# Block 0 of a fused attention and two-layer MoE kernel: weight conversions put in another place of the order

## The chip, the cores and the metric

The kernel runs on one core of one Trainium2 chip. The metric is the device time of one execution in microseconds (us). TensorE (PE), VectorE (DVE), ScalarE (ACT), GpSimd (POOL) and the DMA queue of SyncE (SP) each work through a list of instructions of their own, in the order in which the built program holds it, and wait for one another by semaphores.

## The reference

A sparse attention (four heads with a local window of 32, four with a stride of 32) feeds a gated layer with RMS normalisation, and that a second gated layer. All of it is fp32.

```python
def _attn_ref(q, k, v):                       # 4 x 8 heads x 576 x 64
    scores = scale * np.matmul(q, k.transpose(0, 1, 3, 2))
    rel = pos[:, None] - pos[None, :]
    mask_local = (rel >= 0) & (rel < 32)
    mask_strided = (rel >= 0) & (pos[None, :] % 32 == pos[:, None] % 32)
    masks = np.stack([mask_local if h < H // 2 else mask_strided for h in range(H)], axis=0)
    ...
    return np.matmul(attn, v)

def _moe_ref(x, w_gate, w_val, w_out, rms_g):  # x: 2304 x 512, w: 512 x 1536
    xn = x / rms * rms_g
    g = xn @ w_gate
    silu = g * (1.0 / (1.0 + np.exp(-g)))
    return silu * (xn @ w_val) @ w_out

def _moe2_ref(x, w_a, w_b, w_out):
    return (x @ w_a) * (x @ w_b) @ w_out
```

## The kernel before, in words

The tokens are worked in six blocks of 4 x 96 = 384 (`NB`, `NTB`). For each block the attention gives x, as four pieces of 128 features. A first stage computes, for each of twelve chunks `fc` of 128 hidden features, g = x Wgate and v = x Wval (24 matmuls of 384 columns, since each operand is split into a high part in fp32r and the rest, and three of the four products are taken), h = silu(g / rms) v, and the output sums y (12 matmuls). A second stage after block 5 does the second layer.

The weights arrive in HBM as 64-bit words (the inputs' raw bytes) and are made into the two parts on the chip, in block 0 alone: later blocks keep the gate and value weights `gv` in SBUF, and read the output weights `wo` back from DRAM (`wod`). The **conversion** of a third (128 x 512 numbers) or of a fused pair (128 x 1024) has these steps: `first` on ACT clears a bit pattern of the high word in place (line 134) and makes the three low bits `z` out of the low word (line 139); `second` on DVE joins the two (line 142); `last` casts the high part on ACT (line 147) and subtracts it on POOL (line 148). With a low mode "D" instead of "A" (the table `LOW`), line 136 on DVE makes `z` in place of line 139 on ACT. Chunks 1 to 10 convert gate and value weights as one pair (`FUSEDW`).

Block 0 holds three things at once: its own attention, of which nothing hides the start; the conversions of all weights; and the attention of block 1, whose pieces `attention_slot` puts behind the chunks. Most raw weights have slots of their own; the six last thirds (`wo` of chunks 8 to 11, gate and value of chunk 11) share a pool `raw` of two buffers, so four of their loads wait until the conversion of an earlier third has read its buffer. Behind the last store into `wod` stand the loads of keys for block 2's attention on the same queue.

What sets the order: the program is written in the order of the code, and a scheduler with a model of costs puts each engine's instructions in order before the kernel runs. `tc.issue_after(i)` keeps instructions written inside it behind instruction `i` in that order. `gate(n)` uses it with the n-th row of `GATES`, names of instructions of block 0's attention: `pvm` and `pvr` are the last value product and its sum (lines 278, 281), `sqr` and `snorm` the strided scores' last sum and their normalisation, `norm` the local softmax's, `xhi` the last cast of x, `sqrt` the RMS root (445), `rec` its reciprocal (447). `behind(list)` does the same with a list. `GATES[0]` guards chunk 0's conversion, `GATES[1]` chunk 1's and the first `wo`. The Silu of a chunk is line 751, its product with v line 761, the split of h lines 502 and 503. PSUM tiles of g and v share three banks, so the value product of chunk 1 waits for line 750 of chunk 0 and the gate product of chunk 2 for line 761 of chunk 0.

Of the kernel before, what the change touches and what calls it, by code (L numbers as in the profile page):

```python
# [10 lines left out]
F32 = mybir.dt.float32  # L11
# [4 lines left out]
ALU = mybir.AluOpType  # L16
# [9 lines left out]
NFC = FF // 128  # L26
# [17 lines left out]

GATES = ["pvm snorm sqr",
         "norm pvm snorm sqr",
         "pvr snorm xhi",
         "snorm sqr sqrt xhi",
# [18 lines left out]

LOW = ["AAA"] * NFC
NEG = -1000000000.0
# [5 lines left out]
def fused_kernel(ctx: ExitStack, tc: tile.TileContext, qtl, ktl, vl, qs, ks, vs, cst, w1, w2, out):  # L75
# [5 lines left out]
    nc = tc.nc  # L81
# [102 lines left out]
    def attention(t, pool, psum, banks):  # L184
# [173 lines left out]
        def ptc(g):  # L358
            def f():
                rows, n, keys, units = GROUPS[g]  # L360
                k0 = 0 if g < 2 else 64
                src = st["pps", g][k0:k0 + n].rearrange("k (u h r) -> k u h r", h=2, r=rows // 2)
                for hf in range(2) if g == 2 else [g]:
                    dst = pts[hf][k0:k0 + n, :, :, k0:k0 + rows // 2]
                    nc.scalar.copy(dst, src[:, 4 * hf:4 * hf + 4] if g == 2 else src)
            return f
# [13 lines left out]
        def xhl(i, src):  # L380

            xx = act.tile([128, 2, NTB], F32R, tag="x", name="xx", bufs=8)
            hi, lo = xx[:, 0], xx[:, 1]
            st["xhi"] = nc.scalar.activation(hi, src, AF.Copy, scale=g_sb[:, i:i + 1])
            sq(i)()
            st["xlo"] = nc.vector.scalar_tensor_tensor(lo, src, g_sb[:, i:i + 1], hi.bitcast(F32), op0=ALU.mult, op1=ALU.subtract)
            xt[t, i] = xx
# [99 lines left out]
    def tmp(name):  # L487
        return act.tile([128, NTB], F32, tag="t", name=name, bufs=NTMP)

    made = []  # L490

# [44 lines left out]
    def load_late(which):  # L536
        raw.update(zip(which, load_pair(w1, which, pool)))
# [182 lines left out]
    for t in range(NB):  # L720
# [10 lines left out]
        for fc in range(NFC):  # L731
# [6 lines left out]
            if t == 0 and fc + 1 < NFC:  # L738
                with gate(fc + 1):
                    convert1(fc + 1)  # L740
                if fc + 2 == NFC:
                    load_late([(NFC - 2, 2), (NFC - 1, 2)])
# [20 lines left out]
            if t == 0:  # L763
                wt = wo[0, fc] = wo_tile()
                with gate(fc + 1):
                    run(conversion(raw.pop((fc, 2)), wt, pool, engine(WLO[fc][2]), LOW[fc][2], True))
# [3 lines left out]
                if fc == NFC - 3:  # L770
                    load_late([(NFC - 1, 0), (NFC - 1, 1)])
            prev = (t, fc)
    emit_y(*prev)
# [239 lines left out]
```

## Time and profile before

| what | value |
|---|---|
| median of 3 runs | 982.59 us (980.43, 982.59, 1163.71) |
| the profiled execution's own time | 981.18 us |
| its span, first to last instruction | 979.4 us |
| PE busy, weight loads busy | 944.5 us (96%), 896.9 us (92%) |
| DVE, ACT, POOL busy | 625.2 us (64%), 429.3 us (44%), 537.6 us (55%) |
| mean granted clock of PE | 0.99 |

The page gives the whole span; what the change touches lies in its first 150 us, so it is read there by stretches (windows) and by single instructions in order of time (timelines). A timeline row gives the start, the duration, the engine, the line, the operation, output and inputs, shape and count, and in brackets how long the engine had idled and who ended that. A row of the windows gives the window, its length, then the busy time and instructions of PE, of its weight loads, of DVE, ACT and POOL (of PE and its loads alone, or fewer, where one engine was asked for), the granted clock as a share of the full one, the busy share of the DMA engines and GB/s.

### The profile page before, as it was taken

The numbers are of one execution on the slowest core, as the hardware profiler recorded it, in microseconds if no ns is written. First come the engines' busy times: TensorE is split into PE (matmuls) and PEld (weight loads), VectorE is DVE, ScalarE is ACT, GpSimd is POOL, SyncE is SP. The second block draws the span as 40 slices with busy tenths as digits, with TensorE's granted clock in tenths as the row PEclk, the third lists the DMA queues.
The fourth block names the chain that finished last, engine by engine and source line by source line (L and its number), as shares of the span: only waits on it lengthen the run. The fifth ranks groups of instructions, "written<-read, shape, count | busy, mean of one in ns | idle before, by whom it ended". The sixth has DMA issues, their size and how long they took to land.

```text
span 979.4 us, 14348 instructions
## 1 busy us (share of the span) xinstructions
PE 944.5 (96%) x5438; PEld 896.9 (92%) x5438; DVE 625.2 (64%) x903; ACT 429.3 (44%) x800; POOL 537.6 (55%) x406
## 2 busy tenths in 40 slices
PE   5799999999999999999998999999999999999998
PEld 4699889999999999999998999899999999999996
DVE  5578757648917885887566657666656655465534
ACT  5989645243534433433455555435335423122110
POOL 4488846558739776968346544755643424123211
PEclk7989999999999999999999999999999999999999
DMA  9953376435534553532687975897893973863701
GB/s 347 407 231 119 114 282 210 147 117 177 187 108 134 200 168 110 173 121 80 213 343 302 344 281 206 318 417 319 337 366 138 356 293 113 284 248 150 269 11 65
DMA packets 57364, 215.57 MB, mean 220 GB/s; under 512 B 5968, under 2 KB 14544, under 8 KB 51664
## 3 DMA queue, kind: packets, MB, share of 16 engines
q1 hardware_dynamic: 57296, 214.66, 59.9%
q8 instruction: 43, 0.70, 0.3%
q14 instruction: 25, 0.20, 0.1%
HBM read 172.17 MB, written 42.47 MB: 219 GB/s over the span
## 4 chain that ended last, share of the span: by engine, by line
PE 69%; DVE 10%; DMA 7%; ACT 6%; POOL 4%; issue 4%; SPq 0%; POOLq 0%; DVEq 0%; ACTq 0%
PE o L892 5%; PE o L894 5%; PE o L893 5%; PE Y L838 4%; PE Y L837 4%; PE Y L836 4%; PE y L478 3%; PE v_ps L478 3%; PE y L479 3%; PE y L480 3%; PE v_ps L480 3%; PE g_ps L478 3%; PE v_ps L479 3%; PE g_ps L480 3%; PE g_ps L479 3%
## 5 line engine op out<-in xcount | busy, mean ns | idle before, releaser
L148 POOL TENSOR_TENSOR hl<-c,hl 128x384 fp32r<-128x384 f32 x72 | 79.8, 1109 | 185.7 <-ACT hl L147 180.1
L245 POOL TENSOR_TENSOR prod<-kv_t,qs_t 128x512 f32<-128x512 f32 (+12 forms) x57 | 107.7, 1913 | 17.8 <-DMA kv_t<-in_ks 5.9
L478 PE MATMUL g_ps<-xx,gv 128*128 128x384 f32 x288 | 98.2, 341 | 5.1 <-DVE h L761 5.1
L843 DVE TENSOR_TENSOR c<-c,Y 128x384 f32<-128x384 f32 x108 | 59.3, 551 | 67.5 <-PE Y L838 59.7
L478 PE MATMUL v_ps<-xx,gv 128*128 128x384 f32 x288 | 97.7, 339 | 2.6 <-DVE sg L750 2.1
L479 PE MATMUL y<-hl,wo 128*128 128x384 f32 x288 | 96.1, 338 | 4.0 <-DVE hl L503 4.0
L479 PE MATMUL v_ps<-xx,gv 128*128 128x384 f32 x288 | 98.1, 341 | 0.0
L278 POOL TENSOR_TENSOR prod<-kv_t,S_t 128x512 f32<-128x512 f32 (+12 forms) x57 | 84.8, 1500 | 23.9 <-issue 7.4
L480 PE MATMUL v_ps<-xx,gv 128*128 128x384 f32 x288 | 97.5, 339 | 0.0
L480 PE MATMUL g_ps<-xx,gv 128*128 128x384 f32 x288 | 97.3, 338 | 0.0
L479 PE MATMUL g_ps<-xx,gv 128*128 128x384 f32 x288 | 97.1, 338 | 0.0
L480 PE MATMUL y<-hl,wo 128*128 128x384 f32 x288 | 94.8, 337 | 0.0
L503 POOL TENSOR_TENSOR hl<-h,hl 128x384 fp32r<-128x384 f32 x58 | 62.8, 1083 | 47.8 <-ACT hl L502 41.3
L281 DVE TENSOR_REDUCE xs_t<-prod 128x64 f32<-128x448 f32 (+17 forms) x57 | 85.2, 1515 | 6.0 <-POOL prod L278 5.8
L478 PE MATMUL y<-hl,wo 128*128 128x384 f32 x288 | 85.6, 343 | 1.1 <-ACT wo L147 0.9
L892 PE MATMUL o<-slab,hl 128*128 128x512 f32 x216 | 84.7, 393 | 1.0 <-DVE slab L901 0.5
L893 PE MATMUL o<-slab,hl 128*128 128x512 f32 x216 | 84.6, 392 | 0.0
L894 PE MATMUL o<-slab,hl 128*128 128x512 f32 x216 | 83.5, 395 | 0.0
L147 ACT CAST hl<-c 128x384 fp32r<-128x384 f32 x72 | 37.0, 513 | 104.1 <-DVE c L873 103.9
L751 ACT ACTIVATE sg<-sg 128x384 f32<-128x384 f32 x72 | 37.9, 526 | 90.9 <-DVE sg L750 80.3
L838 PE MATMUL Y<-slab,form 128*128 128x384 f32 x216 | 73.1, 338 | 0.0
L837 PE MATMUL Y<-slab,form 128*128 128x384 f32 x216 | 73.0, 338 | 0.0
(135 smaller groups left out, 2515.5 us busy)
## 6 DMA issues: line engine op xcount, KB each, us to landing
form<-formd SPq DMA_DIRECT2D x32, 1792.0 KB, 10.7
wo<-wod SPq DMA_DIRECT2D x60, 512.0 KB, 3.5
raw<-in_w SPq DMA_DIRECT2D x42, 512.0 KB, 6.9
gv_raw<-in_w SPq DMA_DIRECT2D x30, 512.0 KB, 10.0
formd<-form SPq DMA_DIRECT2D x6, 1792.0 KB, 6.8
formd<-forms SPq DMA_DIRECT2D x6, 1792.0 KB, 11.8
slab<-x2d SPq DMA_DIRECT2D x24, 384.0 KB, 4.5
wod<-wo SPq DMA_DIRECT2D x12, 512.0 KB, 3.3
```

What stands on the lines that cost most here:

```text
L148: lo_eng.tensor_tensor(lo, x, hi.bitcast(F32), op=ALU.subtract)
L245: nc.gpsimd.tensor_tensor(pr, st["ks", g][:, :, :n, :], st["qs"][:, heads(g), mm:mm + 1, :].to_broadcast([128, G, n, D]), op=ALU.mult)
L278: st["pvm"] = nc.gpsimd.tensor_tensor(pr, st["vs", g][:, :, :n, :], st["S"][:, heads(g), mm, :n, None].to_broadcast([128, G, n, D]), op=AL ...
L281: st["pvr"] = nc.vector.tensor_reduce(st["xs"][:, mm, heads(g), :], pr.rearrange("p g n d -> p g d n"), axis=X, op=ALU.add)
L478: nc.tensor.matmul(out_ps, w_hi, x_hi, start=start, stop=False)
L479: nc.tensor.matmul(out_ps, w_hi, x_lo, start=False, stop=False)
L480: nc.tensor.matmul(out_ps, w_lo, x_hi, start=False, stop=stop)
L837: nc.tensor.matmul(bank(n), hi, x[p][:, 1, c], start=False, stop=False, skip_group_check=not begins)
L838: nc.tensor.matmul(bank(n), lo, x[p][:, 0, c], start=False, stop=c == 1, skip_group_check=not begins)
L892: nc.tensor.matmul(o, h[:, 0, cols], w[0], start=n == 0, stop=False)
L893: nc.tensor.matmul(o, h[:, 0, cols], w[1], start=False, stop=False)
L894: nc.tensor.matmul(o, h[:, 1, cols], w[0], start=False, stop=n == len(chunks) - 1)
```

## The change

Five edits. Chunk 0's conversion is also put behind `ptc1`, ACT's copy of the second transposed local weights, and chunk 1's behind `ptc2`, the last of those copies (`GATES`, and `ptc` notes its instruction). Chunk 2's is put behind the RMS root. The low bits of chunks 1 and 2 are made by DVE, for gate and value weights (`LOW`). In `xhl` DVE's low part of x is written ahead of the square. The first `wo` takes row 2 of `GATES` instead of row 1. And every conversion of chunk `fc + 1` and of `wo` `fc` is put behind the product and the split of chunk `fc - 2` (`h_made`).

```diff
--- before.py
+++ after.py
@@ -42,9 +42,9 @@
           "ptc2 pv0 pvc0 pv1 pvc1 xst0 xst1 xstc0 id36 xstc1 rms rinv")
 WARM = 20
 
-GATES = ["pvm snorm sqr",
-         "norm pvm snorm sqr",
-         "pvr snorm xhi",
+GATES = ["pvm snorm sqr ptc1",
+         "norm pvm snorm sqr ptc2",
+         "snorm sqr sqrt xhi",
          "snorm sqr sqrt xhi",
          "rec sexp snorm sqrt xhi"]
 
@@ -65,7 +65,7 @@
 WLO = ["PPP", "PPP", "PPP", "PPP", "PPP", "PPP",
        "PPP", "PPP", "PPP", "PPP", "PPP", "PPD"]
 
-LOW = ["AAA"] * NFC
+LOW = ["AAA", "DDA", "DDA"] + ["AAA"] * 9
 NEG = -1000000000.0
 BIG = 3.0e38
 SCALE = 1.0 / 8.0
@@ -362,7 +362,7 @@
                 src = st["pps", g][k0:k0 + n].rearrange("k (u h r) -> k u h r", h=2, r=rows // 2)
                 for hf in range(2) if g == 2 else [g]:
                     dst = pts[hf][k0:k0 + n, :, :, k0:k0 + rows // 2]
-                    nc.scalar.copy(dst, src[:, 4 * hf:4 * hf + 4] if g == 2 else src)
+                    st[f"ptc{g}"] = nc.scalar.copy(dst, src[:, 4 * hf:4 * hf + 4] if g == 2 else src)
             return f
 
         def pv(p):
@@ -382,8 +382,8 @@
             xx = act.tile([128, 2, NTB], F32R, tag="x", name="xx", bufs=8)
             hi, lo = xx[:, 0], xx[:, 1]
             st["xhi"] = nc.scalar.activation(hi, src, AF.Copy, scale=g_sb[:, i:i + 1])
+            st["xlo"] = nc.vector.scalar_tensor_tensor(lo, src, g_sb[:, i:i + 1], hi.bitcast(F32), op0=ALU.mult, op1=ALU.subtract)
             sq(i)()
-            st["xlo"] = nc.vector.scalar_tensor_tensor(lo, src, g_sb[:, i:i + 1], hi.bitcast(F32), op0=ALU.mult, op1=ALU.subtract)
             xt[t, i] = xx
 
         def xsplit(i, src):
@@ -487,6 +487,7 @@
     def tmp(name):
         return act.tile([128, NTB], F32, tag="t", name=name, bufs=NTMP)
 
+    h_made = {}
     made = []
 
     @contextmanager
@@ -736,7 +737,7 @@
             v_ps = psum.tile([128, 512], F32, tag="gv", name="v_ps", bufs=3)
             mm_in(v_ps[:, :NTB], gv[fc], 1, x)
             if t == 0 and fc + 1 < NFC:
-                with gate(fc + 1):
+                with gate(fc + 1), behind(h_made.get(fc - 2, [])):
                     convert1(fc + 1)
                 if fc + 2 == NFC:
                     load_late([(NFC - 2, 2), (NFC - 1, 2)])
@@ -762,13 +763,15 @@
             hl[t, fc] = split(h, engine(HLO0[fc] if t == 0 else HLO[t]))
             if t == 0:
                 wt = wo[0, fc] = wo_tile()
-                with gate(fc + 1):
+                with gate(max(fc + 1, 2)), behind(h_made.get(fc - 2, [])):
                     run(conversion(raw.pop((fc, 2)), wt, pool, engine(WLO[fc][2]), LOW[fc][2], True))
                 nc.sync.dma_start(wod[fc], wt.rearrange("p a n -> p (a n)").bitcast(F32))
                 if fc % 2:
                     load_units(1)
                 if fc == NFC - 3:
                     load_late([(NFC - 1, 0), (NFC - 1, 1)])
+            if t == 0:
+                h_made[fc] = list(made)
             prev = (t, fc)
     emit_y(*prev)
     evac_y(NB - 1)
```

Where the instructions stand now, at two places. On ACT, behind the square root of the RMS in block 0 (`gv_raw_170` holds the first two `wo` thirds, `173`, `176`, `182`, `185`, `191` the pairs of chunks 1 to 5, `179`, `188` later `wo` thirds; `sg_452` is chunk 0's Silu). Before:

```order
L134 ACTIVATE gv_raw_182<-gv_raw_182 128x1024
L139 ACTIVATE cz_597<-gv_raw_182 128x1024
L134 ACTIVATE gv_raw_179<-gv_raw_179 128x512
L134 ACTIVATE gv_raw_185<-gv_raw_185 128x1024
L139 ACTIVATE cz_684<-gv_raw_185 128x1024
L134 ACTIVATE gv_raw_179<-gv_raw_179 128x512
L134 ACTIVATE gv_raw_188<-gv_raw_188 128x512
L139 ACTIVATE cz_650<-gv_raw_179 128x512
L134 ACTIVATE gv_raw_188<-gv_raw_188 128x512
L134 ACTIVATE gv_raw_191<-gv_raw_191 128x1024
L147 CAST gv_595<-cz_597 128x2x512
L751 ACT_TABLE_LOAD
```

In the changed kernel:

```order
L134 ACTIVATE gv_raw_170<-gv_raw_170 128x512
L139 ACTIVATE cz_481<-gv_raw_170 128x512
L134 ACTIVATE gv_raw_176<-gv_raw_176 128x1024
L134 ACTIVATE gv_raw_170<-gv_raw_170 128x512
L147 CAST wo_479<-cz_481 128x512
L147 CAST gv_513<-cz_515 128x2x512
L752 ACT_TABLE_LOAD
L752 ACTIVATE sg_452<-sg_452 128x384
```

The eleven conversion steps ahead of the Silu's table load have become six, and they are those of the first two `wo` and of chunk 2, which stood ahead of the square root before.

On DVE, at the end of block 0 (`raw_200`, `raw_202`, `raw_1246`, `raw_1248` are the late raw thirds; `prod_1033` and `prod_1133` the last value products of block 1's strided attention, `sg_1198` and `sg_1293` chunks 9 and 10). Before:

```order
L142 SCALAR_TENSOR_TENSOR cz_1159<-raw_200,cz_1159 128x512
L281 TENSOR_REDUCE xs_t_959<-prod_1033 128x128
L750 TENSOR_TENSOR sg_1198<-g_ps_1165,rinv_404 128x384
L435 TENSOR_TENSOR sq_1203<-sq_1203,sq_1063 128x384
L281 TENSOR_REDUCE xs_t_959<-prod_1133 128x128
L761 TENSOR_TENSOR h_1233<-sg_1198,v_ps_1178 128x384
L142 SCALAR_TENSOR_TENSOR cz_1278<-raw_1246,cz_1278 128x512
L503 TENSOR_TENSOR hl_1235<-h_1233,hl_1235 128x384
L142 SCALAR_TENSOR_TENSOR cz_1240<-raw_202,cz_1240 128x512
L750 TENSOR_TENSOR sg_1293<-g_ps_1250,rinv_404 128x384
```

In the changed kernel:

```order
L751 TENSOR_TENSOR sg_1293<-g_ps_1250,rinv_404 128x384
L281 TENSOR_REDUCE xs_t_959<-prod_1033 128x128
L281 TENSOR_REDUCE xs_t_959<-prod_1133 128x128
L435 TENSOR_TENSOR sq_1215<-sq_1215,sq_1203 128x384
L142 SCALAR_TENSOR_TENSOR cz_1159<-raw_200,cz_1159 128x512
L762 TENSOR_TENSOR h_1314<-sg_1293,v_ps_1263 128x384
L447 RECIPROCAL rinv_1300<-rms_t_1298 128x384
L142 SCALAR_TENSOR_TENSOR cz_1240<-raw_202,cz_1240 128x512
L142 SCALAR_TENSOR_TENSOR cz_1278<-raw_1246,cz_1278 128x512
L142 SCALAR_TENSOR_TENSOR cz_1281<-raw_1248,cz_1281 128x512
```

The first join of a late third has moved from ahead of the last two sums (line 281) and of chunk 9's `sg` to behind both sums, chunk 10's `sg` and the last sum of squares, and the others have moved behind the reciprocal.

On PE, the four matmuls that add up the squares for the RMS stand so now: the third behind the 12 matmuls of g of chunk 0, the fourth behind six more of v; before, the last two stood behind seven of each.

## Rows read from the trace of the kernel before

**Rows 1.** Windows by stage: length, busy us (x count) per engine, clock, DMA
```profile
37.98:48.20 10.22, 5.69 (x32) 5.05 (x30) 6.01 (x5) 10.20 (x13) 3.49 (x3) 1.00 1.04 405
48.20:73.60 25.40, 24.23 (x139) 23.91 (x140) 17.75 (x25) 22.59 (x43) 22.16 (x14) 0.87 0.61 236
73.60:98.73 25.13, 24.52 (x166) 23.44 (x165) 21.27 (x27) 23.65 (x44) 22.26 (x15) 1.00 0.33 116
98.73:128.36 29.63, 27.46 (x161) 24.82 (x160) 20.91 (x24) 19.78 (x36) 24.01 (x18) 1.00 0.40 142
...
300.00:400.00 100.00, 100.00 (x630) 98.27 (x629) 81.53 (x105) 39.73 (x64) 77.88 (x49) 1.00 0.45 150
```
**Rows 2.** Window of PE alone after its long pause: length, busy us, clock, DMA
```profile
50.00:52.00 2.00, 2.00 (x8) 0.50 1.08 399
```
**Rows 3.** Timeline of PE: start, us, instruction, [idle before it <- what ended that]
```profile
42.27 0.45 PE L478 MATMUL v_ps<-xx,gv 128*128 128x384 f32 x1 [0.95 <-DVE sg L750]
...
49.37 0.69 PE L478 MATMUL g_ps<-xx,gv 128*128 128x384 f32 x1 [4.75 <-DVE h L761]
...
54.98 0.36 PE L480 MATMUL v_ps<-xx,gv 128*128 128x384 f32 x1
...
57.09 0.33 PE L479 MATMUL g_ps<-xx,gv 128*128 128x384 f32 x1
```
**Rows 4.** Timeline of ACT, from the RMS square root to the first Silu
```profile
37.50 0.58 ACT L445 ACTIVATE rms_t<-att,eps_sb 128x384 f32<-128x384 f32 x1 [0.47 <-PE att L433]
37.98 1.16 ACT L134 ACTIVATE gv_raw<-gv_raw 128x1024 f32<-128x1024 f32 x1
39.00 1.15 ACT L139 ACTIVATE cz<-gv_raw 128x1024 uint32<-128x1024 uint16 x1
...
46.91 1.28 ACT L751 ACT_TABLE_LOAD   x1
48.20 0.52 ACT L751 ACTIVATE sg<-sg 128x384 f32<-128x384 f32 x1
```
**Rows 5.** Timeline of DVE: two joins, x's low parts, the first normalisation
```profile
27.54 1.23 DVE L142 SCALAR_TENSOR_TENSOR cz<-gv_raw,cz 128x1024 uint32<-128x1024 uint32 x1 [1.91 <-ACT cz L139]
...
35.47 1.13 DVE L386 SCALAR_TENSOR_TENSOR xx<-att,cst_sb,xx 128x384 fp32r<-128x384 f32 x2
38.12 2.55 DVE L447 RECIPROCAL rinv<-rms_t 128x384 f32<-128x384 f32 x1 [1.51 <-ACT rms_t L445]
...
41.66 0.55 DVE L750 TENSOR_TENSOR sg<-g_ps,rinv 128x384 f32<-128x384 f32 x1
...
85.39 2.81 DVE L142 SCALAR_TENSOR_TENSOR cz<-gv_raw,cz 128x1024 uint32<-128x1024 uint32 x1
```
**Rows 6.** Groups of DVE by line and shape, 0 to 140 us: xcount | busy us, mean ns | idle before
```profile
L343 DVE TENSOR_SCALAR lsm<-lsm 128x4 f32<-128x4 f32 x4 | 2.4, 594 | 0.0
```
**Rows 7.** Timeline of POOL: first and last value products of the strided attention for block 1
```profile
95.89 2.26 POOL L278 TENSOR_TENSOR prod<-kv_t,S_t 128x512 f32<-128x512 f32 x2 [0.57 <-POOL hl L503]
...
111.31 1.47 POOL L278 TENSOR_TENSOR prod<-kv_t,S_t 128x768 f32<-128x768 f32 x1
```
**Rows 8.** Timeline of DVE at the same place
```profile
111.87 1.46 DVE L142 SCALAR_TENSOR_TENSOR cz<-raw,cz 128x512 uint32<-128x512 uint32 x1 [1.15 <-ACT cz L139]
...
115.77 1.54 DVE L281 TENSOR_REDUCE xs_t<-prod 128x128 f32<-128x768 f32 x1
```
**Rows 9.** Timeline of the DMA queue there, loads of the last raw weights and of block 2's keys
```profile
113.36 0.33 SPq L108 DMA_DIRECT2D raw<-in_w  x1
...
134.98 1.22 SPq L233 DMA_DIRECT2D kv_t<-in_ks  x2
```
**Rows 10.** Timeline of ACT: the first late third that had to wait for its load
```profile
116.97 0.68 ACT L134 ACTIVATE raw<-raw 128x512 f32<-128x512 f32 x1 [1.42 <-DMA raw<-in_w]
```
**Rows 11.** Timeline of PE: first product of block 1 and its first pause
```profile
126.92 0.44 PE L478 MATMUL g_ps<-xx,gv 128*128 128x384 f32 x1
...
144.68 0.45 PE L478 MATMUL v_ps<-xx,gv 128*128 128x384 f32 x1 [1.17 <-DVE sg L750]
```

## The prediction

> **What bounds the kernel now.** I read the windows first. From 300 to 400 us PE is busy all the time [rows 1]. In such a stretch a lead or a lag of PE at the end of block 0 goes straight into the time. The reordered instructions stop differing early in block 2, so the question is only when PE gets block 0 off its hands. In the four windows of block 0, from 37.98 to 128.36 us, PE idles 90.4 - 81.9 = 8.5 us, and it is slowed as well: the granted clock of the second window is 0.87 [rows 1].
>
> The timeline of PE shows where. It waits 4.75 us for chunk 0's product h [rows 3], which waits for the Silu at 48.20 [rows 4]. After that pause the clock stands at 0.50, the lower of the two levels (1.2 GHz) [rows 2]: 17 starts of matmuls from 49.37 to 54.98 take 0.33 us each, then twelve from 54.98 to 57.09 take 0.176 [rows 3]. So the pause costs 4.75 + 17 x 0.154 = 2.6, together 7.4 us. A pause of 0.95 us at 42.27 [rows 3] left no such trace: the clock of the first window is 1.00 [rows 1].
>
> The reader is to see on ACT why the Silu is late. The square root that it needs starts at 37.50, the normalised g is there at 41.66 + 0.55 = 42.2 [rows 5], but ACT does conversions until 46.9 and a table load until 48.2 [rows 4]. In the first window ACT is busy 10.20 of 10.22 us [rows 1].
>
> The other engines are not far behind PE. In the two windows from 48.20 to 98.73 POOL is busy 44.4 and ACT 46.2 of 50.5 us [rows 1]. Whatever is put off at the start has to be done there.
>
> **The sum, first part: the start of block 0.** The square root. 8 us of conversion steps leave ACT's list ahead of it, so ACT alone would allow 29.5. But the third and fourth sum of squares now stand behind 12 and 6 matmuls of chunk 0 on PE, and these need x. The last low part of x ends at 36.60 before [rows 5]; with DVE's earlier sums and ACT's shorter list I put it at 31, an estimate. Then 18 starts of 0.176 = 3.2 and two sums of squares of some 0.8 give 36. With the joins that DVE may do slowly beside POOL (1.23 us for a pair alone, 2.81 beside POOL, [rows 5]) I take 36.7: a gain of 0.8, between 5 at best and -2 if all that is slow.
>
> The first normalisation. The reciprocal takes 2.55 us [rows 5], and behind it DVE now has two joins ahead of `sg`, a third (half of 1.23, so 0.7) and a pair (1.2): 37.3 + 2.55 + 1.9 = 41.7. That is where it was (41.66): nothing gained.
>
> The Silu. Before its table load ACT did, more than now, two pairs' lines 134 and 139 (a start every 1.02 us, from 37.98 to 39.00, [rows 4]) and two thirds' line 134 (half of it): 4 x 1.02 + 2 x 0.5 = 5.1, and one cast of a third less, 0.5. The list is 4.6 us shorter. It would give 48.2 - 0.8 - 4.6 = 42.8, but the last cast ahead of the load waits for the join that ends at 41.7; with a cast of 1.0 and the load of 1.28 the Silu starts at 44.0, 4.2 us earlier. PE's gate product of chunk 2 then starts at about 45.2 instead of 49.37. The pause before it is near 0.8, which I take to leave the clock as the one of 0.95 did, and 2.6 us of slow matmuls fall away. The lead of PE is then 4.2 + 2.6 = 6.8 us; with the clock falling all the same, 4.2.
>
> Line 136, the new operation, has no row. The nearest: a TENSOR_SCALAR on four columns takes 0.59 us in the mean of four [rows 6], far more than its size says; a join of a pair takes 1.23 to 2.81 [rows 5]. I take 1.2 for 1024 columns, between 0.7 (half, and a little) and 2.8. Both stand ahead of the square root, beside PE's wait for x, and are in the 31 above; they take 2 x 1.02 off ACT. The Trainium skill ("VectorE: DVE Perf Modes", the perf-mode tier table) gives fp32 `tensor_scalar` in SBUF two elements a cycle, 1227 ns for 2048; by it line 136 would take an estimated 0.7 us and the front of the sum would come 0.5 us sooner. No run here shows it yet. Swapping line 386 ahead of the square and the gates of chunk 2 add nothing: both stand on instructions that are done by then.
>
> **Second part: the middle pays it back.** What was put off is not saved. Counting ACT's list from the square root to the Silu of chunk 7, before holds one pair's line 139, one third's line 134 and two small copies more, after three third-wide steps more: 2.1 against 1.5 us. So the same work stands ahead of that Silu, whose start before is 98.73 (the end of the third window). ACT idled 60.75 - 56.44 = 4.3 us up to there [rows 1]. At best it comes 0.8 + 0.6 + 4.3 = 5.7 us earlier; with half of that idle time kept, 3.6. POOL has as much to do as before and is busy 22.3 of 25.1 us in the third window. From chunk 5 on I expect PE to wait where it did not before: for a POOL subtraction or for an h whose Silu stands behind exponentials and conversions on ACT, 1 to 1.5 us at a time. The lead is 3.6 us at chunk 7.
>
> **Third part: the end of block 0.** POOL's value products for block 1 cannot start before the strided softmax is normalised, which stays where it was (its exponential follows the same ACT work). Now a `wo` subtraction that waits for its cast stands ahead of them, so I start them at 97.4 instead of 95.89 [rows 7]. From the first product's start to the last one's end, at 111.31 + 1.47 = 112.8, POOL took 16.9 us [rows 7], with one pair, two `wo`, one h and two x between the products. Now one pair and one h more and one `wo` and one x less stand there, about the same: the last ends at 114.4.
>
> Behind it in DVE's new order stand the last sum (1.54, [rows 8]), a transpose and a square for x, the third sum of squares (about 1.2) and only then the first join of a late third. I get its end at 119.5; before it ended at 111.87 + 1.46 = 113.3 [rows 8]. That is 6.2 us later, and on it hang a load (issued at 113.36, [rows 9], used at 116.97, [rows 10]: 3.6 us), the next conversion, the next load, and so on to the keys of block 2, issued at 134.98 [rows 9]: a chain of 21.6 us before. It holds slack that closes now: two loads of 3.6, two times 134 and 139 at 1.1, joins at 0.7, a wait for the reciprocal to about 123.6, a cast, a subtraction and a store. From 119.5 it comes to 123.6 + 0.7 (join 2, load 4 of value weights) + 3.6 + 1.1 + 0.7 = 129.7, then the last load 3.6, 1.1, 0.7, 0.6, 0.7 and three issues of 0.3: 137.3. The keys are 2.3 us late.
>
> For PE: chunk 11's value weights, whose high part is cast at about 130.2, stand ahead of block 1's first product in its list. That starts at about 130.6 instead of 126.92 [rows 11]. So the lead of 3.6 us has become a lag of 3.7. From there PE has the same work left, and the pause of 1.17 at 144.68 [rows 11], a wait for DVE behind the keys' products, closes up, since that `sg` now stands ahead of those sums in DVE's order. A lag of about 2 us is left, which agrees with the keys' 2.3.
>
> **Sum.** Start -6.8, paid back in the middle +3.2, the late thirds' chain +7.3, the pause of block 1 -1.2 and a little of the next: +2. On the profiled execution's 981.18 us that is 983 us. The median of the runs shown, 982.59, is 1.4 above it, so forecast and median are equal within what a measurement of this kernel can tell from no change, about 2%, or 20 us.
>
> **The rivals.** First, the lead is kept. If the late thirds' joins are not on the path (DVE reaches them while PE is still in chunk 9), PE starts block 1 with 3.6 to 6.8 us in hand: 981.2 - 6 = 975. For it: PE was 100% busy in the middle before, so its work there could simply slide forward. Against it: DVE's order puts those joins behind the last sum, and PE's list puts chunk 11 behind them.
>
> Second, slower: each chunk's conversion now follows two chunks' h, so POOL's subtraction of a pair comes just in time. If PE waits w for it in each of eight chunks, 3 to 10, the loss beyond the lead is 8w - 6.8. At w = 2.1 it is 10 us, 991. Over 2% it would be from w = 3.3, more than a pair's subtraction of 2.4 takes, with all else as before. For it: POOL is the fullest engine beside PE. Against it: a pair is cast almost a full chunk of PE's work (36 x 0.176 = 6.3 us) ahead of need. A clock that falls in such waits would add to it.
>
> Third, the change does nothing to the start, because the square root waits for x as before (36.6 to 37.5) and PE's clock falls in a pause of two small pieces: then the lag of the third part stands alone, 985 to 989.
>
> **How the numbers follow.** Forecast (979 to 988, third rival within it at its upper end): 0.56. Lead kept, 970 to 978: 0.20. Just in time, 989 to 1004: 0.22; the rest for neither. The range leaves out the upper part of the slow case and the lower edge of the fast one: 973 to 995. Faster by over 2% would need 20 us where PE's whole loss in block 0 is 8.5 idle and 2.6 slow: 0.02. Slower by over 2%: 0.04. Within: 0.94.
>
> **What would show it.** Right: the first Silu at 44, no window near 0.5 of clock behind it; PE pausing from chunk 5 on for POOL or for h; the first join of a late third at 118 to 120; the keys of block 2 at 136 to 138; block 1's first gate product at 129 to 132. Wrong: that product before 124 (lead kept), or pauses of over 2 us in each of chunks 3 to 10, or a window at half clock between 40 and 60 us.

## The result, and the profile of the kernel after

The changed kernel takes 990.87 us in the median of 4 runs (989.38 to 992.87), against 982.92 us for the kernel before in the same comparison. The ratio is 1.0088 with a 95% interval of 1.0071 to 1.0106: 8 us slower. The forecast was 983.0 us, range 973 to 995, within 2% of before. The time lies in the range because the range is wide. It is outside the 979 to 988 us that the prediction gave as its own forecast, and inside the 989 to 1004 that it gave to the rival "just in time" with a chance of 0.22; the forecast of hardly any change was wrong by 8 us. Of the runs before, one of 1163.71 us is a disturbed one and is left out of the ratio.

The profiled execution took 989.38 us, with a span of 987.2 us. The stages again, with the limits of [rows 1] and one short window more (132 to 134); the columns are length, then busy us (and count) of PE, PEld, DVE, ACT and POOL, then the granted clock, the DMA share and GB/s:

```profile
37.98:48.20 10.22, 7.30 (x40) 6.49 (x39) 6.31 (x7) 9.12 (x13) 5.26 (x3) 1.00 1.04 407
48.20:73.60 25.40, 24.77 (x157) 23.99 (x156) 20.08 (x24) 24.66 (x46) 21.86 (x13) 1.00 0.49 179
73.60:98.73 25.13, 21.34 (x138) 19.87 (x137) 18.70 (x28) 24.95 (x48) 19.72 (x12) 1.00 0.44 154
98.73:128.36 29.63, 24.59 (x129) 20.70 (x127) 22.08 (x20) 18.66 (x34) 26.18 (x19) 0.88 0.23 87
132.00:134.00 2.00, 2.00 (x8) 2.00 (x8) 0.00 (x0) 0.47 (x1) 1.12 (x1) 0.50 1.01 354
300.00:400.00 100.00, 100.00 (x629) 97.97 (x628) 75.25 (x93) 38.60 (x64) 75.13 (x48) 1.00 0.47 155
```

The start did what it should: in the first window PE is busy 7.30 us in place of 5.69, and in the second its clock is 1.00 in place of 0.87. The loss stands in the third and fourth window. In the third PE idles 25.13 - 21.34 = 3.8 us, before 0.6, while ACT is busy all but 0.2 us. In the fourth PE idles 5.0 us (before 2.2) and its clock falls to 0.88 (before 1.00). From 300 us on PE is full, as before, so what is lost by then stays lost.

The timeline of PE shows what it waits for (start, us, instruction, in brackets the idle time ahead of it and what ended that):

```profile
43.25 0.44 PE L478 MATMUL v_ps<-xx,gv 128*128 128x384 f32 x1 [2.25 <-DVE sg L751]
46.29 0.45 PE L478 MATMUL g_ps<-xx,gv 128*128 128x384 f32 x1 [0.68 <-DVE h L762]
...
78.55 0.44 PE L480 MATMUL g_ps<-xx,gv 128*128 128x384 f32 x1 [1.22 <-POOL gv L148]
84.63 0.41 PE L478 MATMUL g_ps<-xx,gv 128*128 128x384 f32 x1 [2.33 <-DVE h L762]
...
113.39 0.44 PE L480 MATMUL g_ps<-xx,gv 128*128 128x384 f32 x1 [1.56 <-POOL gv L148]
...
130.58 0.44 PE L478 MATMUL y<-hl,wo 128*128 128x384 f32 x1 [2.11 <-ACT wo L147]
...
137.13 0.34 PE L478 MATMUL g_ps<-xx,gv 128*128 128x384 f32 x1
```

The pause of 4.75 us [rows 3] has become one of 0.68. The last line is block 1's first product: 137.13 in place of 126.92 [rows 11], 10.2 us late. On ACT the square root and the first Silu (37.50 and 48.20 in [rows 4]):

```profile
37.88 0.58 ACT L445 ACTIVATE rms_t<-att,eps_sb 128x384 f32<-128x384 f32 x1 [4.42 <-PE att L433]
...
45.12 0.53 ACT L752 ACTIVATE sg<-sg 128x384 f32<-128x384 f32 x1
```

The first Silu is 3.1 us earlier. The reader is to see the 4.42 us in the first line as well: ACT stands idle there, where in before it did conversions up to 0.47 us ahead of the square root. DVE at the end of block 0 (before: [rows 8]) and POOL's value products and last subtractions (before: [rows 7]):

```profile
118.85 2.68 DVE L281 TENSOR_REDUCE xs_t<-prod 128x128 f32<-128x640 f32 x2
122.95 0.56 DVE L435 TENSOR_TENSOR sq<-sq 128x384 f32<-128x384 f32 x1 [1.42 <-ACT sq L429]
123.50 0.69 DVE L142 SCALAR_TENSOR_TENSOR cz<-raw,cz 128x512 uint32<-128x512 uint32 x1
```
```profile
98.08 1.30 POOL L148 TENSOR_TENSOR wo<-cz,wo 128x512 fp32r<-128x512 f32 x1 [4.95 <-ACT wo L147]
99.34 2.27 POOL L278 TENSOR_TENSOR prod<-kv_t,S_t 128x512 f32<-128x512 f32 x2
...
114.59 3.46 POOL L278 TENSOR_TENSOR prod<-kv_t,S_t 128x640 f32<-128x640 f32 x2
...
119.31 1.28 POOL L148 TENSOR_TENSOR wo<-cz,wo 128x512 fp32r<-128x512 f32 x1
...
136.69 1.31 POOL L148 TENSOR_TENSOR gv<-cz,gv 128x512 fp32r<-128x512 f32 x1 [3.57 <-ACT gv L147]
```

The first join of a late third starts at 123.50, 11.6 us later than in [rows 8]. The subtraction at 136.69 is the last of chunk 11's value weights; in before it started at 126.26:

```profile
126.26 1.29 POOL L148 TENSOR_TENSOR gv<-cz,gv 128x512 fp32r<-128x512 f32 x1 [2.59 <-ACT gv L147]
```

The DMA queue follows (before: [rows 9]):

```profile
124.22 0.33 SPq L108 DMA_DIRECT2D raw<-in_w  x1
...
144.48 1.70 SPq L233 DMA_DIRECT2D kv_t<-in_ks  x3
```

A walk along the Silus of block 0 shows when the lead is lost. The changed kernel is ahead by 3.1 us at the first, 0.2 at the fourth (59.71 against 59.95), 3.9 at the fifth (69.72 against 73.60), 6.3 at the ninth (100.39 against 106.67), 2.4 at the eleventh (118.96 against 121.38). At the twelfth, that of chunk 11, it is 6.0 behind, and at block 2's first Silu 7.7, which is about the difference of the two spans, 7.8. Before:

```profile
131.98 0.53 ACT L751 ACTIVATE sg<-sg 128x384 f32<-128x384 f32 x1 [0.21 <-DVE sg L750]
...
223.27 0.53 ACT L751 ACTIVATE sg<-sg 128x384 f32<-128x384 f32 x1 [1.14 <-DVE sg L750]
```

In the changed kernel:

```profile
137.93 0.53 ACT L752 ACTIVATE sg<-sg 128x384 f32<-128x384 f32 x1
...
230.97 0.53 ACT L752 ACTIVATE sg<-sg 128x384 f32<-128x384 f32 x1 [1.14 <-DVE sg L751]
```

### The profile page after: what moved, and what is told of

Its sections match the earlier page's. It is cut to its first block, busy times and chain, and to the rows that moved or that the text cites. A ratio compares the mean times of both kernels' runs of the same rounds, so it can differ in the third digit from the quotient of the medians.

```text
span 987.2 us, 14357 instructions
## 1 busy us (share of the span) xinstructions
PE 951.3 (96%) x5438; PEld 900.4 (91%) x5438; DVE 629.3 (64%) x905; ACT 427.5 (43%) x798; POOL 539.3 (55%) x406
## 4 chain that ended last, share of the span: by engine, by line
PE 75%; DVE 9%; ACT 7%; issue 4%; DMA 3%; POOL 2%; SPq 0%; POOLq 0%; DVEq 0%; ACTq 0%
PE o L895 5%; PE o L897 5%; PE o L896 5%; PE Y L841 4%; PE Y L840 4%; PE Y L839 4%; PE v_ps L478 4%; PE y L478 4%; PE v_ps L480 4%; PE y L479 3%; PE v_ps L479 3%; PE y L480 3%; PE g_ps L478 3%; PE g_ps L480 3%; PE g_ps L479 3%
## 5 line engine op out<-in xcount | busy, mean ns | idle before, releaser
L479 PE MATMUL y<-hl,wo 128*128 128x384 f32 x288 | 98.2, 342 | 3.8 <-DVE hl L504 3.8
L478 PE MATMUL g_ps<-xx,gv 128*128 128x384 f32 x288 | 97.4, 338 | 3.7 <-DVE h L762 3.7
L480 PE MATMUL y<-hl,wo 128*128 128x384 f32 x288 | 93.9, 338 | 0.0
L478 PE MATMUL y<-hl,wo 128*128 128x384 f32 x288 | 89.3, 349 | 4.4 <-ACT wo L147 4.0
L504 POOL TENSOR_TENSOR hl<-h,hl 128x384 fp32r<-128x384 f32 x58 | 65.8, 1134 | 47.4 <-ACT hl L503 40.9
## 6 DMA issues: line engine op xcount, KB each, us to landing
gv_raw<-in_w SPq DMA_DIRECT2D x30, 512.0 KB, 10.2
```

The lines of the kernel that those rows point to most:

```text
L478: nc.tensor.matmul(out_ps, w_hi, x_hi, start=start, stop=False)
L479: nc.tensor.matmul(out_ps, w_hi, x_lo, start=False, stop=False)
L480: nc.tensor.matmul(out_ps, w_lo, x_hi, start=False, stop=stop)
```

## The experiments

**Theory 1**: the loss is the chain of late thirds. The first join of a late third comes late, a load, a conversion and a load hang on it, and chunk 11's weights and block 1 come late. **Rival 2**: conversions that come just in time make PE pause in the middle of block 0, and that is the loss. **Rival 3**: line 136 on DVE costs more than it frees. Every edit lets the scheduler place other instructions anew, so each run is read in its trace and not by its time alone.

**Run 1: the kernel before, with the late join held back.**
```
-                with gate(fc + 1):
+                with gate(fc + 1), tc.issue_after(nxt["st"]["pvr"].ins) if fc == 8 else nullcontext():
```


> The kernel before, with one order added: the first join of a late third (chunk 8's output weights, 111.87 in the trace of before) waits on VectorE behind the last sum of the value products (115.77 to 117.3). Nothing else of the change is in it. Theory 1 (what the change costs is the late thirds' chain through two buffers, set by where that join stands): the join comes at 116 to 118, the raw load behind it, block 1's first product of gates and the keys of block 2 all slip by 4 to 6 us, and the time is 986 to 989. Rival 2 (the pauses of TensorE in the middle of block 0, for conversions made just in time) and rival 3 (ScalarE's step given to VectorE for two chunks) hold nothing here: 982 to 984, as before.

Measured: 983.4 us, ratio 1.0003 (0.9990 to 1.0017). DVE's join and POOL's last subtraction for chunk 11:
```profile
115.91 1.02 DVE L142 SCALAR_TENSOR_TENSOR cz<-raw,cz 128x512 uint32<-128x512 uint32 x1
```
```profile
129.68 1.30 POOL L148 TENSOR_TENSOR gv<-cz,gv 128x512 fp32r<-128x512 f32 x1 [1.28 <-ACT gv L147]
```
The join came 4.0 us later (111.87 in [rows 8]) and chunk 11's last subtraction 3.4 later, and it cost nothing; this run's trace stands some 1.3 us later from the square root on (38.85), so the edit itself moved the join by 2.7. Theory 1 as it was written, which expected 3 to 6 us for this, falls: the chain has some 2 to 3 us of slack in before. A delay as long as the 11.6 us of after was not tried. In this run the reciprocal came ahead of the second half of the chain (125.82 in place of 128.98), which may be part of that slack.

**Run 2: after, without the two waits behind h.**
```
-                with gate(fc + 1), behind(h_made.get(fc - 2, [])):
+                with gate(fc + 1):
...
-                with gate(max(fc + 1, 2)), behind(h_made.get(fc - 2, [])):
+                with gate(max(fc + 1, 2)):
```


> The kernel after the change without its two waits behind the h of two chunks earlier; the new gates, the two chunks on VectorE and the swapped square stay. On VectorE the first late join still stands behind the last sum and the third sum of squares. Theory 1 with the join's place as the cause: still slow, 988 to 992, with the first late join at 121 to 124. Theory 1 with the waits as the cause, and rival 2 (those waits make conversions come just in time): 981 to 985, TensorE's pauses at 78, 85 and 103 us gone. Rival 3: 990, no change.

Measured: 995.97 us, ratio 1.0135 (1.0107 to 1.0163). Slower than either theory had it. With the new gates in place, the waits don't cause the loss; without them it is larger. The first Silu comes at 50.21, the join at 126.96. Rival 2's form "those waits make the conversions late" falls for this kernel; run 12 comes back to it.

**Run 3: after, without line 136.**
```
-LOW = ["AAA", "DDA", "DDA"] + ["AAA"] * 9
+LOW = ["AAA"] * NFC
```


> The kernel after the change with the low words of chunks 1 and 2 back on ScalarE. Rival 3 (the step on VectorE, 1.75 us beside GpSimd, and the shifts behind it cost the loss): 984 to 987. Theory 1: 989 to 993, since the first late join stays behind the third sum of squares; the first Silu moves by at most 1 us, and the second of chunk 1 comes up to 1 us later.

Measured: 999.89 us, ratio 1.0158 (1.0130 to 1.0187). Rival 3 falls, the other way round: two steps of 1.1 us given back to ACT make the changed kernel 9 us slower. None of the theories had that. It pointed to ACT's load; but the order is made anew as well, and runs 7 and 8 show that ACT's load alone doesn't set the time.

**Run 4: after, with the late join two places earlier on DVE.**
```
...
+            if t == 0 and fc >= 8:
+                convert2(fc, False)
             if nxt is not None:
-                attention_slot(nxt, fc)
+                with tc.issue_after(joined[0]) if t == 0 and fc == 8 else nullcontext():
+                    attention_slot(nxt, fc)
...
```
Here `convert2` is the conversion of one chunk's output weights, called from this place for chunks 8 to 11 and without the wait behind h, and `joined` holds its join.

> The kernel after the change, with the output weights of chunks 8 to 11 converted without the wait behind h and issued ahead of the attention's slot of their chunk, and the last sum of the value products held behind the first late join. On VectorE the join stands two places earlier, ahead of the last sum and of the third sum of squares. Theory 1: the first late join comes at 119 to 121 in place of 123.5, the raw loads and block 1's start follow by 2 to 5 us, time 986 to 989. Rivals 2 and 3: 990 to 992, and block 1's own attention (its reciprocal at 126.8) later by the time the sum waits.

Measured: 987.21 us, ratio 1.0040 (1.0026 to 1.0054), 3.7 us better than after. The join comes at 120.80. Ahead of it, its line 141 (139 in after) on ACT had waited 1.13 us for POOL's subtraction of the output weights before them, since these conversions share one buffer. So theory 1 was narrowed: each conversion of output weights waits for POOL to finish the one ahead, and chunk 11 stands behind them.

**Run 5: after, with that subtraction on DVE for chunks 4 to 11** (chunk 11's was there already).
```
-WLO = ["PPP", "PPP", "PPP", "PPP", "PPP", "PPP",
-       "PPP", "PPP", "PPP", "PPP", "PPP", "PPD"]
+WLO = ["PPP"] * 4 + ["PPD"] * 8
```


> The kernel after the change, with the low half of the output weights (line 148) of chunks 4 to 11 taken off GpSimd and given to VectorE (0.69 us there in the trace of before, 1.28 on GpSimd), which frees the one buffer of these conversions sooner. Theory 1, narrowed by the first runs (each output-weight conversion waits for the buffer that GpSimd's last cast of the one before it frees, and chunk 11's gate and value weights wait behind them for raw buffers): the last cast of chunk 11's weights comes at 127 to 132 in place of 136.7, time 981 to 986. Rival 2 (the pauses in the middle): 989 to 992. A rival 5, that VectorE is now the fuller engine: 991 or more, with its joins later.

Measured: 985.9 us, ratio 1.0034 (1.0020 to 1.0048). Chunk 11's last subtraction (this kernel's lines stand one lower than after's), and the fourth window:
```profile
129.27 1.28 POOL L147 TENSOR_TENSOR gv<-cz,gv 128x512 fp32r<-128x512 f32 x1 [3.46 <-ACT gv L146]
```
```profile
98.73:128.36 29.63, 25.41 (x153) 23.07 (x152) 25.37 (x25) 19.48 (x36) 21.44 (x14) 0.94 0.36 125
```
It is 7.4 us earlier than in after and 5 us come back, not 8: inside the range expected by theory 1, at its upper end. The edit also takes work off POOL (21.44 us in this window, 26.18 in after) and gives it to DVE (25.37, in after 22.08), so it doesn't tell the buffer from POOL's load.

**Run 6: before, with the new table of gates alone.**
```
-GATES = ["pvm snorm sqr",
-         "norm pvm snorm sqr",
-         "pvr snorm xhi",
+GATES = ["pvm snorm sqr ptc1",
+         "norm pvm snorm sqr ptc2",
+         "snorm sqr sqrt xhi",
...
```


> The kernel before with the new table of gates alone (and the names of the transposed copies that it waits on). Theory 1: the conversions that went ahead of the attention now come behind it, ScalarE is some 8 us behind with them, and nothing pays it back: 993 to 1003, first Silu at 44 to 46 or 50 to 51, last cast of chunk 11's weights at 139 or later. Rival: the gates cost little and the two waits behind h and the rest of the change are what delays: 981 to 986.

Measured: 991.1 us, ratio 1.0084 (1.0063 to 1.0105), as much as the whole change. That is 2 us less than theory 1 had it, and the last subtraction comes at 136.81, as in after. There is no earlier start in it: the first Silu stands at 49.43.

**Run 7: before, with line 136 for chunks 1 to 5.**
```
-LOW = ["AAA"] * NFC
+LOW = ["AAA"] + ["DDA"] * 5 + ["AAA"] * 6
```


> The kernel before with line 139's step of the gate and value weights of chunks 1 to 5 on VectorE (line 136) in place of ScalarE, and nothing else. Five times 1.13 us leave ScalarE, which is busy 22.6 of 25.6 us and 23.7 of 25.1 us in the two stages after the first Silu. Theory 1 with ScalarE's backlog as its source: 976 to 981. If VectorE, slowed beside GpSimd, is as full: 982 to 986.

Measured: 982.84 us, ratio 1.0002 (0.9988 to 1.0016); the gain expected by theory 1 is not there. The kernel was 3.3 us ahead at the tenth Silu (111.71 against 115.02), and lost it where PE waits for chunk 11:
```profile
126.71 0.45 PE L478 MATMUL v_ps<-xx,gv 128*128 128x384 f32 x1 [1.62 <-ACT gv L147]
...
128.06 0.69 PE L480 MATMUL v_ps<-xx,gv 128*128 128x384 f32 x1 [0.73 <-POOL gv L148]
```
The last subtraction is at 126.73, as in before. At the ninth Silu the lead was 0.3 us (106.35 against 106.67), at the eleventh 2.2 (119.16 against 121.38), at the twelfth it was gone (132.45 against 131.98). So here too a lead ends at chunk 11's weights, though nothing was put off.

**Run 8: after, with line 136 for chunks 1 to 5.** The same line of the table as in run 7, put into the kernel after.

> The kernel after the change with line 139's step on VectorE for chunks 1 to 5 in place of 1 and 2 only. Taking it back to ScalarE for two chunks cost 9 us. Theory 1 with ScalarE's backlog as its source: three chunks more give 3 to 9 us, 981 to 987, last cast of chunk 11's weights at 128 to 134. If VectorE takes over as the bound: 990 to 995.

Measured: 992.32 us, ratio 1.0106 (1.0084 to 1.0128). Three chunks more don't help after; PE now waits 5.64 us for a cast of ACT at 86.85. The expectation of 3 to 9 us was a miss: the 9 us of run 3 can't be scaled by the number of steps.

**Run 9: after, with the late output weights in other buffers.**
```
-    run(conversion(raw.pop((fc, 2)), wt, pool, engine(WLO[fc][2]), LOW[fc][2], True))
+    run(conversion(raw.pop((fc, 2)), wt, pool, engine(WLO[fc][2]), LOW[fc][2], fc < 8))
```


> The kernel after the change, with one argument altered: the output weights of chunks 8 to 11 are converted in the two buffers of the gate and value weights in place of the one buffer that the output weights share. Nothing is left out. The first late join then needn't wait for GpSimd's last cast of chunk 7's output weights. Theory 1 (the loss is the backlog of output weights in their one buffer, which chunk 11's weights wait behind): the first late join comes at 100 to 106 in place of 123.5, the last cast of chunk 11's weights at 120 to 128 in place of 136.7, time 978 to 984. Rival 2 (pauses in the middle of block 0): 988 to 992, since these stay. A rival 6, that chunk 11's weights only wait elsewhere (GpSimd, VectorE): last cast at 130 or later, 985 to 990.

Measured: 986.54 us, ratio 1.0035 (1.0022 to 1.0048). DVE's first late join and POOL's last subtraction:
```profile
98.06 0.69 DVE L142 SCALAR_TENSOR_TENSOR cz<-raw,cz 128x512 uint32<-128x512 uint32 x1 [0.66 <-ACT cz L139]
```
```profile
130.04 1.29 POOL L148 TENSOR_TENSOR gv<-cz,gv 128x512 fp32r<-128x512 f32 x1 [1.28 <-ACT gv L147]
```
The join is 25 us earlier than in after, yet the last subtraction only 6.7 and the time 4.3. Opening this buffer gives half of the loss back. The other half stays, and the last subtraction comes at 130 all the same, as rival 6 had it. POOL is busy 28.22 of 29.63 us from 98.73 to 128.36 (before 24.01, [rows 1]); but in run 5, where about as much of the loss stays, it is busy only 21.44, so a full POOL is not the whole reason. That window in run 9:
```profile
98.73:128.36 29.63, 25.23 (x152) 21.50 (x151) 23.10 (x23) 20.11 (x36) 28.22 (x20) 1.00 0.35 110
```

**Runs 10 and 11: the same argument in the kernel before, alone and with run 7's table.**

> The kernel before with the same one argument altered, so that chunks 8 to 11's output weights use the two buffers of the gate and value weights. In before, TensorE waits for chunk 11's second cast (126.26) by 0.5 us only and the reciprocal holds the Silu of chunk 11 (131.98). Theory 1: a small gain, 977 to 982, last cast of chunk 11's weights at 112 to 121. If the conversions taken early delay chunks 9 and 10: 983 to 986.

> The kernel before with both: line 139's step of chunks 1 to 5 on VectorE, and the free buffer for chunks 8 to 11. With the first alone block 0 ran 3.3 us ahead at chunk 9's Silu and lost it on TensorE's wait for chunk 11's value weights (1.62 and 0.73 us, and a halved clock behind them). Theory 1: the lead is kept, 975 to 980. If the lead is lost elsewhere: 982 to 985.

Measured: 983.75 us, ratio 1.0004 (0.9992 to 1.0016), and 981.75 us, ratio 0.9990 (0.9978 to 1.0001). The last subtraction came 4.7 and 2.2 us earlier than in before (121.59 and 124.04) and gave nothing that can be told from no change, where theory 1 expected 1 to 8 us. In before the chain isn't the bound. No run is faster than before by more than its interval.

**Run 12: after, with the old table of gates.** Run 6's diff, taken out of the kernel after.

> The kernel after the change with the old table of gates; all else of the change stays (two chunks' step on VectorE, the swapped square, the output weights from the third gate on, the two waits behind h). The gates alone gave 991. Theory 1 (what was put behind the attention's end is work that ScalarE and GpSimd can't do later without falling behind): the conversions of chunk 2 and of the first output weights go ahead of the root of the mean square again, ScalarE is busy 19 to 25 us of the first 38 in place of 17.6, last cast of chunk 11's weights at 124 to 130, time 979 to 985. If the waits behind h and the rest cost by themselves: 986 to 991.

Measured: 993.26 us, ratio 1.0102 (1.0079 to 1.0124), a miss. The gates alone cost the whole loss, and the change without them costs it too. The windows up to 48 us show what the two have in common, for before, after and run 12 in turn:
```profile
0.00:48.00 48.00, 32.64 (x214) 27.72 (x214) 26.37 (x48) 35.22 (x64) 20.32 (x19) 0.86 0.98 376
```
```profile
0.00:48.00 48.00, 37.17 (x223) 31.27 (x224) 25.60 (x49) 26.54 (x54) 18.90 (x18) 0.79 0.98 375
```
```profile
0.00:48.00 48.00, 34.95 (x210) 29.77 (x211) 27.45 (x49) 26.06 (x54) 19.26 (x19) 0.81 0.98 379
```
ACT, the fourth engine of the row, did 35.2 us of work by 48 us in before and 26.5 and 26.1 in the others. Two steps of some 1.1 us had moved to DVE; the rest, 6.5 to 7 us, was put off: call it ACT's debt. In run 12 it isn't the gates that put it off. The conversions that they hold are done ahead of the square root (42.09) again: POOL subtracts the first two output weights at 34.80 and 39.77, and chunk 2's pair at 36.12 (before: 26.33, 38.93 and 36.59). But ACT starts on chunk 3's pair only at 47.52 (before at 37.98), right behind the split of chunk 0's h, which is where the wait behind h of two chunks earlier puts it:
```profile
47.10 0.51 ACT L503 CAST hl<-h 128x384 fp32r<-128x384 f32 x1 [0.62 <-DVE h L762]
47.52 1.17 ACT L134 ACTIVATE gv_raw<-gv_raw 128x1024 f32<-128x1024 f32 x1
```
So the trace has the waits behind h putting work off in run 12, as the gates do in run 6; taking out only one of the two (runs 2 and 12) keeps the loss. The same reading of all kernels (each line 136 that DVE had done by then counted as 1.1 us of ACT's work):

| kernel | ACT's work by 48 us | start of chunk 11's last subtraction | block 2's first Silu | median us |
|---|---|---|---|---|
| before | 35.2 | 126.26 | 223.27 | 982.92 |
| run 1 | 33.9 | 129.68 | 224.96 | 983.4 |
| run 7 | 34.7 | 126.73 | 222.85 | 982.84 |
| run 10 | 35.0 | 121.59 | 223.41 | 983.75 |
| run 11 | 35.1 | 124.04 | 225.09 | 981.75 |
| run 5 | 28.6 | 129.27 | 226.45 | 985.9 |
| run 9 | 28.8 | 130.04 | 227.17 | 986.54 |
| run 4 | 29.8 | 133.22 | 227.04 | 987.21 |
| after | 28.7 | 136.69 | 230.97 | 990.87 |
| run 6 | 30.8 | 136.81 | 232.39 | 991.1 |
| run 8 | 29.7 | 138.60 | 233.95 | 992.32 |
| run 12 | 28.3 | 135.44 | 232.25 | 993.26 |
| run 2 | 29.9 | 141.64 | 236.22 | 995.97 |
| run 3 | 28.1 | 141.57 | 239.90 | 999.89 |

The 1.3 us by which run 1's whole trace is late are most of its shortfall in the second column. (Each run had its own runs of before beside it, with medians from 982.25 to 983.45.) The kernels fall into two groups. All five that had done 33.9 us or more of ACT's work by 48 us take the time of before, whatever else was changed. All nine that had done 28 to 31 are slower, by 3 to 17 us. Within these the debt doesn't order the times (run 6 put off least and is slower than four others); the last subtraction does so nearly, though runs 12 and 3 stand out: where it comes after about 130, each further us costs about one. All five of the first group keep before's gates and have no waits behind h, and all nine of the second have at least one of these two edits. So the table can't tell ACT's debt from whatever else these edits do to the order.

## Why the prediction came out as it did

**The start was right.** Predicted: first Silu at 44.0, no window near half clock behind it. Measured: 45.12, and the clock of the second window is 1.00. Some 0.9 us of the difference was there early: the exponential of block 0's strided attention starts at 16.10 in after's trace and at 15.18 in before's. In run 4, which has the start of after, it stands at 15.11, and the first Silu at 44.12. The square root, predicted at 36.7, stands at 37.88 here (37.50 in before) and at 36.89 in run 4. What holds it is the last sum of squares on PE behind 18 products, as the first part had it, and not x, as in the third rival: x's last low part ends at 32.2, 4.4 us earlier than in before, and PE's products start only at 33.13.
```profile
31.07 1.14 DVE L385 SCALAR_TENSOR_TENSOR xx<-att,cst_sb,xx 128x384 fp32r<-128x384 f32 x2 [0.32 <-ACT xx L384]
```
```profile
33.13 0.42 PE L478 MATMUL g_ps<-xx,gv 128*128 128x384 f32 x1
```
ACT's shorter list behind the root gave the gain, as the sum said.

**Line 136** was taken at 1.2 us between 0.7 and 2.8. It took 1.75 and 0.69:
```profile
26.01 1.75 DVE L136 TENSOR_SCALAR cz<-gv_raw 128x1024 uint32<-128x1024 uint32 x1 [0.41 <-POOL gv L148]
...
29.54 0.69 DVE L136 TENSOR_SCALAR cz<-gv_raw 128x1024 uint32<-128x1024 uint32 x1
```
The first ran while POOL's subtraction (24.70 to 27.21) did, the second alone. The estimate of 0.7 from the Trainium skill ("VectorE: DVE Perf Modes", the perf-mode tier table) agrees with the second. For the first, the Trainium skill ("SBUF — State Buffer", "SBUF: two separate sides") says that DVE in a two-port perf mode and GpSimd share one pair of ports as an exclusive lock: whichever starts first has it for its whole instruction, and the other blocks. The trace agrees nearly, since the 1.75 us end 0.55 behind POOL's end, against 0.69 for the shift alone.

**The middle was right in kind.** Predicted: pauses of 1 to 1.5 us from chunk 5 on for POOL or for h, a lead of 3.6 at chunk 7. Measured: 1.22 at 78.55 for POOL, 2.33 at 84.63 for h, and a lead of 2.6 at chunk 7's Silu (96.17 against 98.73). The sentence "what was put off is not saved" was right and stopped too early. It took the debt as settled at chunk 7, with the list ahead of that Silu nearly as long as before. The list was: from the square root to that Silu ACT was busy 56.92 us in before and 56.31 in after. The debt was not settled. Up to 98.73, in before and in after:
```profile
0.00:98.73 98.73, 81.38 (x517) 75.07 (x518) 65.39 (x98) 81.66 (x151) 64.95 (x46) 0.90 0.72 274
```
```profile
0.00:98.73 98.73, 83.48 (x515) 75.34 (x516) 64.38 (x100) 76.35 (x145) 60.66 (x42) 0.90 0.72 268
```
With 2.2 us for the two steps that DVE does, ACT still owed 81.66 - 78.55 = 3.1 of the 6.5 us, and POOL 4.3. What was owed were the output weights: at 98.08 POOL starts on the low half of chunk 5's, where before, at 98.12, it started on chunk 6's. Its lag at these weights was 4.2 us at chunk 4 (86.23 against 82.03), and from there it grew, to 7.4 at chunk 5 (98.08 against 90.69) and 11.8 at chunk 7 (119.31 against 107.55).

**The third part failed, by its size.** It sized the chain at +7.3, from a lead of 3.6 at chunk 7 to a lag of 3.7 at block 1's first product. Measured are 12.8, from a lead of 2.6 to a lag of 10.2. The final lag was to be 2; it is 7.7. Its places:

| place | before | predicted | after |
|---|---|---|---|
| first value product on POOL | 95.89 | 97.4 | 99.34 |
| last value product ends | 112.8 | 114.4 | 118.05 |
| first late join starts | 111.87 | 118.8 | 123.50 |
| block 1's first product | 126.92 | 130.6 | 137.13 |
| block 2's keys issued | 134.98 | 137.3 | 144.48 |

(The prediction gave the end of the join, 119.5; 0.7 is taken off.) The first two rows miss by 1.9 and 3.7. POOL stood idle for 4.95 us ahead of 98.08, waiting for ACT's cast of chunk 5's output weights: the debt, that the second part had as paid. Between the products stood just what the prediction had counted, but a pair and an h for an output weight and an x is 2.34 + 1.32 in place of 1.29 + 1.01, 1.4 us more and not "about the same". The third row misses by 4.7, since DVE waits for these products in order, and since chunk 7's output weights leave the one buffer only with POOL's subtraction from 119.31 to 120.6. The second join then waits for the reciprocal to 129.3 (126.78 + 2.55), not to 123.6, and PE's clock is at half from 132 to 134 (0.50); the last two rows miss by 6.5 and 7.2. The credit for block 1's pause was about right: 10.2 at its first product has become 7.7.

Runs 4, 5 and 9 show that this chain is part of the loss: three ways of making it shorter give 3.7, 5.0 and 4.3 of the 8 us. Run 1 shows what the prediction had wrong in it: in before, the join may come some 3 us later at no cost. The prediction explained the chain by the order on DVE; the runs point to the work put off on ACT, and with it on POOL, as the source, without showing it alone.

**The rivals.** "Lead kept" was refuted in the trace: it was kept to the ninth Silu and lost behind it. "Just in time" told of pauses that are there (3.8 us of idle PE in the third window; 0.63, 1.22, 1.22 and 1.56 us for conversions at 70.80, 78.55, 103.52 and 113.39, and 2.33 for h at 84.63). They are fewer, and but for the one for h shorter, than the 2.1 us in each of eight chunks that this rival needed for 991, so the time in its range doesn't bear it out. The 3 to 4 us that are left in runs 5 and 9, where chunk 11's last subtraction comes at about the 130 that cost run 1 nothing, may be theirs. That was not shown.

**What stays open.** Why a debt of 4 to 7 us costs 3 us in one order and 17 in another isn't settled; the last subtraction of chunk 11 tells most of it, but runs 12 and 3 show that it doesn't tell all. In run 12 ACT was busy 4.31 of the 10 us from 38 to 48, and the square root came at 42.09; the trace points to the waits behind h, but no run takes them out with the old gates and the rest of the change in place. That the debt is the cause rests on 14 kernels falling into two groups, which the edits divide in the same way; no run took the debt alone away from the changed kernel.

## What to carry to other kernels

Work that fills an engine's wait is free where it stands. What these runs suggest, though they don't show it alone: moved behind the wait, into a stretch in which that engine is 90% busy (ACT, 46.2 of 50.5 us), it becomes a debt that shows up later, here 80 us later in the last chunk. So count, for each engine, the work done by the end of the quiet stretch, in both orders, and follow the difference until it is paid, the least urgent work first, because that is what slips. And test a chain from both sides: lengthening it in the good kernel (run 1) showed slack that shortening it in the bad one (runs 4, 5, 9) could not.

## What the runs showed of the hardware

One shift of 1024 columns on DVE took 0.69 us alone and 1.75 beside a subtraction of POOL; two places for the same instruction 3.5 us apart differ by a factor of 2.5. In after's trace PE's clock stayed at 1.00 through pauses of 2.25 us at 43.25 and 2.33 at 84.63, and stood at 0.50, the lower level of 1.2 GHz, from 132 to 134, behind a pause of 2.11, and already from 114 to 116, behind one of 1.56 at 113.39:
```profile
114.00:116.00 2.00, 2.00 (x8) 0.50 0.01 4
```
The length of the pause alone doesn't tell: in run 9 the same pause of 2.25, at 43.22, goes with a clock of 0.83 from 38 to 48 us.
